# First two token groups transposed on TensorE, the other transposes issued by SyncE, attention units respaced

## Chip, cores and metric

The kernel runs on one core of one Trainium2 chip. The metric is the device time of one launch in microseconds (us), the median of several runs. Engines in the listings: PE is TensorE (matmuls), PEld its weight loads, DVE is VectorE, ACT is ScalarE, POOL is GpSimd, SP is SyncE. A "q" behind a name (ACTq, SPq) is the engine's instruction queue issuing a DMA. L213 is line 213 of the kernel; the change adds lines, so line numbers differ between the two kernels.

## The reference, cut to what matters

Four layers over x of shape 1 x 2048 x 1024, bf16: A, B, A, B, each behind a layer norm and added back to x.

```python
# A: linear attention, 32 heads of 32
q, k, v = split(layernorm(x) @ wqkv)               # 1024 -> 3 x 1024
phi = lambda t: where(t > 0, t + 1, exp(t)) + 1e-6
kv, z = sum_s(phi(k) * v), sum_s(phi(k))           # per head
x = x + ((phi(q) @ kv) / (phi(q) @ z + 1e-6)) @ wo
# B: gated block, F = 3584
x = x + ((h @ w_gate) * (h @ w_up)) @ w_down       # h = layernorm(x)
```

## The kernel before

2048 tokens are 16 tiles of 128, in four groups (g = 0 to 3) of four tiles. The matmuls of this kernel contract over the partitions, so each normalised tile `xn` (tokens on partitions) has to be transposed into `xT` (features on partitions), and each attention output tile `onat` into `oT`. All these transposes are DMAs issued from ScalarE's queue:

```python
def transpose_tile(src, dst):
    nc.scalar.dma_start_transpose(out=dst, in_=src)

def phi(ps, dst):                       # evicts a k or q output
    e = eb[phis[0] % 3]; phis[0] += 1
    nc.scalar.activation(out=e, in_=ps[:], func=ACT.Exp)
    nc.vector.tensor_scalar(out=e, ...)                 # min, add
    nc.vector.scalar_tensor_tensor(out=dst, in0=ps[:], in1=e, ...)

def mm_tile():                          # four PSUM banks for matmul outputs
    return psum.tile([P, NB], F32, tag="mm", bufs=4, name="ps")

def kv_tile():                          # four banks, one buffer
    return psum.tile([P, KD, ZS], F32, tag="kv", bufs=1, name="kv")
# ... cut
def layer_A(li):
    ones()
    if li == 0:
        for t in range(TPG):
            ln_stats(t)
            if t > 0: ln_apply(t - 1)
        ln_apply(3)
        for t in range(TPG):
            tx(t, 0)()                  # DMA transpose of tile t
            k_unit(t, 0)()              # 8 matmuls, then phi
        # ... main: the other k, v and kv units of group 0
        do(weave(main, norm_fill(1, 1, True), 1, 1))
    # ... cut: kv groups 1 to 3, q groups 0 and 1
    do(kv_group(3) + [kv_unit(NT - 1)])
    load_gu(0); load_gu(1)
    f0 = o_fill(0)                      # o units and oT transposes of group 0
    do(weave(q_group(2), [f0[i] for i in (0, 1, 3, 5)], 1, 2))
    do(weave(q_group(3), [f0[i] for i in (2, 4, 6, 7)], 0, 2))
    load_gu(2)
    do(weave(out_group(0), o_fill(1), 0, 1))
    do(weave(out_group(1), [stats_unit(t) for t in range(TPG)] + o_fill(2), 0, 1))
    do(weave(out_group(2), o_fill(3), 0, 1))
    do(weave(out_group(3), norm_fill(0, 0, False), 0, 1))

def layer_B(li):
    load_d()                            # seven 1 MB loads of w_down, on SyncE
    # ... gate/up units, then down units, per group
```

Units are closures that are emitted in list order; each engine works through its own share in that order (at the start of layer 2, below, ScalarE's exps stand behind its transposes until 884.89 us). An o unit is eight small matmuls (128x132) into the single `kv` buffer and a VectorE eviction (L266 before, L281 after). All plain loads are issued by SyncE.

## Time and profile before

The time is 1715.66 us. The floor of TensorE can be worked out from the trace: at full clock eight 128x512 matmuls take 1.727 us and eight 128x132 ones 0.47 us; 7424 of the first and 512 of the second make 1632 us. So about 83 us are lost, and the question is where.

The page of the kernel before: the span, each engine's busy time, TensorE's busy tenths and granted clock in 40 slices, and the chain of waits by engine.

```profile
span 1715.2 us, 18587 instructions
...
PE 1648.8 (96%) x7794; PEld 761.7 (44%) x7952; DVE 538.9 (31%) x963; ACT 246.1 (14%) x418; POOL 53.5 (3%) x150
...
PE   3999998999999999999979999989999999999999
...
PEclk7999999999999999999989999999999999999999
...
PE 94%; DVE 3%; DMA 2%; issue 1%; ACTq 0%; ACT 0%; POOL 0%; POOLq 0%
```

TensorE is the bound; the first slice (43 us) is 30% busy, and there are dents at slices 7, 21 and 27: before layer 1, at the start of layer 2 and before layer 3. TensorE's list of waits in the kernel before: its line and tile, what ended the wait, us in total, how many waits, the longest.

```profile
PE ps L213 <- DMA xT_70<-xn: 24.9, 4, 9.5
PE ps L213 <- ACT H L226: 10.7, 1, 10.7
PE kv L261 <- DVE H L266: 8.1, 8, 2.1
PE ps L301 <- DMA xT_70<-xn: 4.3, 1, 4.3
PE ps L301 <- issue: 4.3, 1, 4.3
```

Five groups of waits, in four places. (For the last line the profile names no releaser; it is the step into layer 3, the same place as the line above it has in layer 1.) The first is the start; its timeline (start us, us, engine, line, operation, and in brackets the idle time before and what ended it):

```profile
6.85 1.42 ACTq L177 DMA_TRANSPOSE xT_70<-xn  x1
...
15.95 3.60 PE L213 MATMUL ps<-W_74,xT_70 128*128 128x512 bf16 x8 [9.51 <-DMA xT_70<-xn]
...
19.58 0.60 ACT L203 ACTIVATE H<-ps 128x512 bf16<-128x512 f32 x1 [17.36 <-PE ps L213]
19.65 1.25 ACTq L177 DMA_TRANSPOSE xT_70<-xn  x1
...
28.56 3.50 PE L213 MATMUL ps<-W_74,xT_70 128*128 128x512 bf16 x8 [9.02 <-DMA xT_70<-xn]
```

The first two transposes take 9 us each to land among the initial loads (the other two 3 us), and each after the first is issued only after ScalarE has done the exp of the tile before. Eight matmuls take 3.5 us here, twice the full-clock time.

The second is the start of layer 2 in the kernel before:

```profile
873.94 1.89 PE L223 MATMUL ps<-W_77,xT_70 128*128 128x512 bf16 x8
...
877.11 7.74 ACTq L177 DMA_TRANSPOSE xT_72<-xn  x4
...
884.89 1.08 ACT L203 ACTIVATE H<-ps 128x512 bf16<-128x512 f32 x2 [65.42 <-DMA xT_72<-xn]
...
885.85 0.69 DVE L205 SCALAR_TENSOR_TENSOR H<-ps,H 128x512 bf16<-128x512 f32 x1
885.86 1.08 ACT L226 CAST H<-ps 128x512 bf16<-128x512 f32 x2
...
886.51 1.44 PE L213 MATMUL ps<-W_74,xT_70 128*128 128x512 bf16 x3 [10.68 <-ACT H L226]
```

In ScalarE's order four transposes stand before the exps. The first k output is complete by 870.65 us (868.76 plus 1.89), but ScalarE waits until 877.11 us for VectorE's normalised tiles, then sits in the four issues, and starts the exp at 884.89. Meanwhile two k and two v outputs fill the four PSUM banks. TensorE's fifth output waits 10.68 us.

The third place is the step into the gate/up matmuls of layers 1 and 3.

```profile
278.91 0.54 DVE L172 TENSOR_SCALAR xn<-X,mv,rstd 128x1024 bf16<-128x1024 bf16 x1
...
280.02 0.37 SPq L95 DMA_DIRECT2D D_78<-in_B_w_down_dram  x1
...
286.06 1.44 PE L301 MATMUL ps<-xT_70,W_74 128*128 128x512 bf16 x3 [4.34 <-DMA xT_70<-xn]
```

The last tile of group 0 is normalised at 279.45 us; its transpose lands 6.6 us later. The fourth place is the attention tail of each A layer, where o units wait for VectorE's eviction of the single kv buffer (L266, 8.1 us in all).

### The profile page before, as it was taken

Reading aid. Unit: us, or ns where it says so; the run is one execution under the profiler, and the core shown is the slowest. Engines: PE = TensorE matmul, PEld = TensorE weight load, DVE = VectorE, ACT = ScalarE, POOL = GpSimd, SP = SyncE. Lnnn points to the kernel's source line nnn. Section 1 sums busy time; section 2 is a strip of 40 time slices with the busy share of each in tenths; the row PEclk is TensorE's granted clock in tenths of the full one; section 3 lists DMA queues with packets and bytes.
Section 4 is the critical chain, followed back from the end, with each engine's and each line's share of the span. In section 5 each row is a group of like instructions: output and inputs, shape, how many; then the busy total and the mean of one; then the engine's idle time right before and its main releaser. Section 6 shows DMA issues by size and latency. Waiting matters only on the chain.

```text
span 1715.2 us, 18587 instructions
## 1 busy us (share of the span) xinstructions
PE 1648.8 (96%) x7794; PEld 761.7 (44%) x7952; DVE 538.9 (31%) x963; ACT 246.1 (14%) x418; POOL 53.5 (3%) x150
## 2 busy tenths in 40 slices
PE   3999998999999999999979999989999999999999
PEld 1444444444444444444434444434444444444444
DVE  2553674321321221132342337742113113111211
ACT  0333300110110011011013332001101101100110
POOL 1100000000000000000110000000000000000000
PEclk7999999999999999999989999999999999999999
DMA  8310447641453164053250015376406424531400
GB/s 263 93 26 13 144 79 207 186 151 46 112 158 99 49 172 147 1 161 109 62 145 16 1 43 148 56 245 174 152 19 172 147 68 116 160 108 63 149 4 22
DMA packets 248900, 183.67 MB, mean 107 GB/s; under 512 B 104432, under 2 KB 239600, under 8 KB 248816
## 3 DMA queue, kind: packets, MB, share of 16 engines
q1 hardware_dynamic: 147440, 157.30, 29.0%
q10 hardware_dynamic: 101376, 25.18, 8.2%
q8 instruction: 62, 1.02, 0.2%
q14 instruction: 22, 0.18, 0.0%
HBM read 153.09 MB, written 4.19 MB: 92 GB/s over the span
## 4 chain that ended last, share of the span: by engine, by line
PE 94%; DVE 3%; DMA 2%; issue 1%; ACTq 0%; ACT 0%; POOL 0%; POOLq 0%
PE ps L301 45%; PE ps L313 22%; PE ps L213 7%; PE ps L250 6%; PE ps L223 6%; PE ps L287 5%; DMA xT_70<-xn 2%; DVE st L158 1%; PE kv L237 1%; PE kv L261 1%; DVE X L279 1%; DVE H L266 1%; ACTq L177 0%; DVE mv L160 0%; DVE den L265 0%
## 5 line engine op out<-in xcount | busy, mean ns | idle before, releaser
L305 DVE TENSOR_TENSOR H<-gs,ps 128x512 bf16<-128x512 f32 x224 | 154.0, 688 | 580.9 <-PE ps L301 559.7
L304 ACT COPY gs<-ps 128x512 f32<-128x512 f32 x224 | 131.0, 585 | 1076.8 <-PE ps L301 951.8
L313 PEld LDWEIGHTS <-H 128*128 128x128 bf16 x1792 | 175.4, 98 | 211.4
L279 DVE TENSOR_TENSOR X<-X,ps 128x512 bf16<-128x512 bf16 x128 | 87.4, 683 | 361.4 <-PE ps L313 330.4
L203 ACT ACTIVATE H<-ps 128x512 bf16<-128x512 f32 x128 | 76.3, 597 | 252.9 <-PE ps L213 89.1
L204 DVE TENSOR_SCALAR H<-H 128x512 bf16<-128x512 bf16 x128 | 37.3, 291 | 203.1 <-ACT H L203 203.1
L301 PEld LDWEIGHTS <-W_74 128*128 128x128 bf16 x640 | 62.9, 98 | 85.7 <-issue 11.5
L301 PEld LDWEIGHTS <-W_75 128*128 128x128 bf16 x640 | 63.2, 99 | 77.6 <-issue 3.6
L301 PEld LDWEIGHTS <-xT_73 128*128 128x128 bf16 x576 | 56.4, 98 | 67.9
L301 PEld LDWEIGHTS <-W_77 128*128 128x128 bf16 x576 | 56.4, 98 | 67.9
L301 PEld LDWEIGHTS <-W_76 128*128 128x128 bf16 x576 | 56.4, 98 | 68.0
L301 PEld LDWEIGHTS <-xT_72 128*128 128x128 bf16 x576 | 56.4, 98 | 68.0
L301 PE MATMUL ps<-xT_70,W_74 128*128 128x512 bf16 x314 | 77.0, 388 | 8.9 <-DMA xT_70<-xn 4.3
L158 DVE BATCH_NORM_STATS2 st<-X 128x6 f32<-128x512 bf16 x128 | 80.9, 674 | 5.1 <-DMA X<-in_A_x_dram 5.1
L301 PE MATMUL ps<-xT_70,W_75 128*128 128x512 bf16 x316 | 76.7, 386 | 0.2
L301 PE MATMUL ps<-xT_70,xT_73 128*128 128x512 bf16 x314 | 75.3, 379 | 0.3
L301 PE MATMUL ps<-xT_70,xT_72 128*128 128x512 bf16 x314 | 75.3, 379 | 0.3
L301 PE MATMUL ps<-xT_71,W_77 128*128 128x512 bf16 x314 | 75.3, 379 | 0.3
L301 PE MATMUL ps<-xT_71,W_76 128*128 128x512 bf16 x310 | 75.1, 379 | 0.5
L287 PEld LDWEIGHTS <-H 128*128 128x128 bf16 x512 | 49.9, 99 | 57.0 <-issue 3.0
L301 PE MATMUL ps<-xT_71,W_75 128*128 128x512 bf16 x314 | 74.6, 379 | 0.4
L301 PE MATMUL ps<-xT_71,W_74 128*128 128x512 bf16 x314 | 74.3, 379 | 0.2
(82 smaller groups left out, 1701.1 us busy)
## 6 DMA issues: line engine op xcount, KB each, us to landing
W_74<-in_B_w_gate_dram SPq DMA_DIRECT2D x20, 1024.0 KB, 5.5
W_75<-in_B_w_up_dram SPq DMA_DIRECT2D x20, 1024.0 KB, 7.7
W_76<-in_B_w_gate_dram SPq DMA_DIRECT2D x18, 1024.0 KB, 5.6
W_77<-in_B_w_up_dram SPq DMA_DIRECT2D x18, 1024.0 KB, 7.7
xT_72<-in_B_w_gate_dram SPq DMA_DIRECT2D x18, 1024.0 KB, 5.3
xT_73<-in_B_w_up_dram SPq DMA_DIRECT2D x18, 1024.0 KB, 7.2
X<-in_A_x_dram SPq DMA_DIRECT2D x16, 256.0 KB, 7.3
out_dram<-X SPq DMA_DIRECT2D x32, 128.0 KB, 1.7
```

The lines of the kernel that those rows point to most:

```text
L158: nc.vector.bn_stats(out=st[:, c, :], in_=X[:, t, c * NB:(c + 1) * NB])
L203: nc.scalar.activation(out=e, in_=ps[:], func=ACT.Exp)
L204: nc.vector.tensor_scalar(out=e, in0=e, scalar1=1.0, scalar2=1e-6, op0=ALU.min, op1=ALU.add)
L213: nc.tensor.matmul(out=ps[:], lhsT=xt[:, k, tl * P:(tl + 1) * P], rhs=wk[n][:, k, :], start=(k == 0), stop=(k == KD - 1))
L223: nc.tensor.matmul(out=ps[:], lhsT=xt[:, k, tl * P:(tl + 1) * P], rhs=wv[n][:, k, :], start=(k == 0), stop=(k == KD - 1))
L250: nc.tensor.matmul(out=ps[:], lhsT=wq[n][:, k, cl * P:(cl + 1) * P], rhs=xT[g][:, k, :], start=(k == 0), stop=(k == KD - 1))
L279: nc.vector.tensor_tensor(out=X[:, t, n * NB:(n + 1) * NB], in0=X[:, t, n * NB:(n + 1) * NB], in1=ps[:], op=ALU.add)
L287: nc.tensor.matmul(out=ps[:], lhsT=oT[(t // TPG) % 2][:, c, tl * P:(tl + 1) * P], rhs=wo[n][:, c, :], start=(c == 0), stop=(c == KD - 1))
L301: nc.tensor.matmul(out=ps[:], lhsT=w[:, k, j * P:(j + 1) * P], rhs=xT[g % 2][:, k, :], start=(k == 0), stop=(k == KD - 1))
L304: nc.scalar.copy(out=gs[:], in_=gp[:])
L305: nc.vector.tensor_tensor(out=hT[:, f, :], in0=gs[:], in1=up[:], op=ALU.mult)
L313: nc.tensor.matmul(out=ps[:], lhsT=hT[:, f, tl * P:(tl + 1) * P], rhs=wd[f][:, n * NB:(n + 1) * NB], start=(f == 0), stop=(f == KF - 1))
```

## The change

Its intent: (1) at the start, transpose groups 0 and 1 on TensorE itself, with a ScalarE copy out of PSUM, instead of waiting for DMAs that stand among the loads; (2) take all other transposes out of ScalarE's queue; (3) spread the o units, transposes and norm units so that none waits for the single kv buffer, and normalise the next layer's first group one output group earlier. The core of the diff:

```diff
-    for k in range(0, KD, 4):
-        load(wk[0][:, k:k + 4, :], wqkv_v[:, k:k + 4, D:D + NB])
+    for k in range(0, KD, 2):
+        load(wk[0][:, k:k + 2, :], wqkv_v[:, k:k + 2, D:D + NB])
 ... (identity added; the mask is built after the first statistics)
     def transpose_tile(src, dst):
-        nc.scalar.dma_start_transpose(out=dst, in_=src)
+        nc.sync.dma_start_transpose(out=dst, in_=src)
 ...
+    def tx_pe(t):
+        def run():
+            if t not in xns:
+                ln_apply(t)
+            src = xns.pop(t)
+            pt = psum.tile([P, KD, P], BF16, tag="mm", bufs=MM, name="pt")
+            for k in range(KD):
+                nc.tensor.transpose(out=pt[:, k, :], in_=src[:, k * P:(k + 1) * P], identity=ident[:])
+            nc.scalar.copy(out=xT[t // TPG][:, :, t % TPG * P:(t % TPG + 1) * P], in_=pt[:])
+        return run
 ... layer_A, li == 0
+            tx_pe(0)()
             for t in range(TPG):
-                tx(t, 0)()
                 k_unit(t, 0)()
+                if t < 3:
+                    tx_pe(t + 1)()
 ...
-            do(weave(main, norm_fill(1, 1, True), 1, 1))
+            fill = []
+            for t in range(TPG, 2 * TPG):
+                fill += [stats_unit(t), apply_unit(t), tx_pe(t)]
+            do(weave(main, fill, 1, 1))
 ... attention tail (the old one is printed above)
+        do([q2[0], kv_unit(NT - 1), q2[1], q2[2], o0[0], q2[3], q2[4], o0[1], t0[0], q2[5], o0[2], t0[1], q2[6],
+            q2[7], o0[3], t0[2], q3[0], q3[1], q3[2], o1[0], t0[3], q3[3], q3[4], o1[1], t1[0], q3[5],
+            q3[6], o1[2], t1[1], q3[7]])
 ... then output groups 0 and 1 with the other o units and the statistics
+        load_gu(2)
+        u = out_group(2)
+        do([t3[0], t3[1], u[0], o3[3], t3[2], u[1], a[0], u[2], t3[3], x[0], u[3], a[1], u[4], x[1], u[5], a[2],
+            u[6], x[2], u[7], a[3]])
+        do([x[3]] + out_group(3))
```

More of the change, by code (lines that the diff above doesn't have):

```diff
@@ L6 @@
 from concourse._compat import with_exitstack
+from concourse.masks import make_identity
 ACT = mybir.ActivationFunctionType
@@ L134, with make_mask @@
     load_o()
-    mask = const.tile([P, ZW], F32, tag="mask", name="mask")
-    nc.gpsimd.memset(mask[:], 0.0)
-    for b in range(HC):
-        nc.gpsimd.memset(mask[32 * b:32 * b + 32, 32 * b:32 * b + 32], 1.0)
-        nc.gpsimd.memset(mask[32 * b:32 * b + 32, P + b:P + b + 1], 1.0)
+    ident = const.tile([P, P], BF16, tag="ident", name="ident")
+    make_identity(nc, ident[:])
     mhalf = const.tile([P, 1], F32, tag="mhalf", name="mhalf")
     nc.gpsimd.memset(mhalf[:], -0.5)
+    mask = const.tile([P, ZW], F32, tag="mask", name="mask")
+    def make_mask():
+        nc.gpsimd.memset(mask[:], 0.0)
+        for b in range(HC):
+            nc.gpsimd.memset(mask[32 * b:32 * b + 32, 32 * b:32 * b + 32], 1.0)
+            nc.gpsimd.memset(mask[32 * b:32 * b + 32, P + b:P + b + 1], 1.0)
     warm = const.tile([P, 1], F32, tag="warm", name="warm")
@@ L186, in tx @@
         return run
-    def tx_group(g, slot):
-        return [tx(g * TPG + tl, slot) for tl in range(TPG)]
+    def tx_pe(t):
[8 more added lines that the diff above has]
+        return run
     def mm_tile():
@@ L355, in layer_A @@
     def layer_A(li):
-        ones()
         if li == 0:
@@ L362, in layer_A @@
             ln_apply(3)
+            ones()
+            make_mask()
+            tx_pe(0)()
             for t in range(TPG):
-                tx(t, 0)()
                 k_unit(t, 0)()
+                if t < 3:
+                    tx_pe(t + 1)()
             ts = range(TPG)
@@ L371, in layer_A @@
                     main.append(kv_unit(t - 1))
-            do(weave(main, norm_fill(1, 1, True), 1, 1))
+            fill = []
+            for t in range(TPG, 2 * TPG):
+                fill += [stats_unit(t), apply_unit(t), tx_pe(t)]
+            do(weave(main, fill, 1, 1))
         else:
+            ones()
             do(weave(kv_group(0), norm_fill(3, 3, False), 1, 2))
@@ L378, in layer_A, with o, to @@
         do(q_group(1))
-        do(kv_group(3) + [kv_unit(NT - 1)])
+        do(kv_group(3))
         load_gu(0)
         load_gu(1)
-        def o_fill(g):
-            o = [o_unit(t) for t in range(g * TPG, (g + 1) * TPG)]
-            tr = [to_unit(t) for t in range(g * TPG, (g + 1) * TPG)]
-            return [o[0], o[1], tr[0], o[2], tr[1], o[3], tr[2], tr[3]]
+        def o(g):
+            return [o_unit(t) for t in range(g * TPG, (g + 1) * TPG)]
+        def to(g):
+            return [to_unit(t) for t in range(g * TPG, (g + 1) * TPG)]
         def out_group(g):
             return [u for t in range(g * TPG, (g + 1) * TPG) for u in (out_unit(t, 0), out_unit(t, 1))]
-        f0 = o_fill(0)
-        do(weave(q_group(2), [f0[i] for i in (0, 1, 3, 5)], 1, 2))
-        do(weave(q_group(3), [f0[i] for i in (2, 4, 6, 7)], 0, 2))
+        o0, t0, o1, t1, o2, t2, o3, t3 = o(0), to(0), o(1), to(1), o(2), to(2), o(3), to(3)
+        q2, q3 = q_group(2), q_group(3)
+        do([q2[0], kv_unit(NT - 1), q2[1], q2[2], o0[0], q2[3], q2[4], o0[1], t0[0], q2[5], o0[2], t0[1], q2[6],
+            q2[7], o0[3], t0[2], q3[0], q3[1], q3[2], o1[0], t0[3], q3[3], q3[4], o1[1], t1[0], q3[5],
+            q3[6], o1[2], t1[1], q3[7]])
+        s = [stats_unit(t) for t in range(TPG)]
+        a = [apply_unit(t) for t in range(TPG)]
+        x = [tx(t, 0) for t in range(TPG)]
+        u = out_group(0)
+        do([u[0], o1[3], t1[2], u[1], u[2], o2[0], t1[3], u[3], u[4], o2[1], u[5], u[6], o2[2], u[7]])
+        u = out_group(1)
+        do([t2[0], t2[1], t2[2], u[0], o2[3], u[1], t2[3], s[0], u[2], o3[0], u[3], s[1], u[4], o3[1], u[5], s[2],
+            u[6], o3[2], u[7], s[3]])
         load_gu(2)
-        do(weave(out_group(0), o_fill(1), 0, 1))
-        do(weave(out_group(1), [stats_unit(t) for t in range(TPG)] + o_fill(2), 0, 1))
-        do(weave(out_group(2), o_fill(3), 0, 1))
-        do(weave(out_group(3), norm_fill(0, 0, False), 0, 1))
+        u = out_group(2)
+        do([t3[0], t3[1], u[0], o3[3], t3[2], u[1], a[0], u[2], t3[3], x[0], u[3], a[1], u[4], x[1], u[5], a[2],
+            u[6], x[2], u[7], a[3]])
+        do([x[3]] + out_group(3))
     def layer_B(li):
```

## The prediction

> What bounds it now. TensorE: 96% of the 1715.2 us span in the page, 94% of the chain of waits. At full clock eight 128x512 matmuls take 1.727 us in the timeline (0.216 each), eight 128x132 ones 0.47. So 7424 of the first and 512 of the second need 1632 us. The other 83 us are TensorE idle or at half cadence (0.427 us a matmul). From its timeline:
> (a) Layer 0 start: the first 32 matmuls of k end at 45.4 us; 6.9 us of work. Waits on xT transposes by DMA: 24.9 us in the list of waits. ScalarE issues each transpose behind the exp of the tile before, and the first two take 9 us to land among the weight loads.
> (b) Attention tail, each A layer: waits for the eviction L266 of 0.34, 1.39, 2.06, about 0.3 us, 0.49 in the last kv unit, about 1.5 us of half clock: some 6 us each.
> (c) Into layers 1 and 3: 4.3 us for the last xT_70 transpose, then half clock: 6.9 and 6.0 us.
> (d) Layer 2 start: 10.7 us idle. ScalarE sits in four transpose issues (877 to 885 us) before it can evict the PSUM banks; then 2.7 us at half clock.
> The last 3.5 us are the final add and store.
>
> What the change does.
> (a) 64 TensorE transposes, 0.06 to 0.11 us each (estimate from the 128x132 matmuls; the Trainium skill, "TensorE: Matmul & The Clock Gate", Part 4, says they don't engage the clock gate; no trace here shows it). A tile costs about 0.6 us plus one ScalarE copy, estimated at 1.05 us from 0.585 for 128x512. xn of tile 0 is there at 6.8 us, tile 1 at 11.5, tiles 2 and 3 at 13.4 and 14.7. Per tile transpose, copy, eight matmuls: 3.6 us warm, 5.5 cold. The 32 matmuls end at 22 to 29 us instead of 45.4; I take 20 saved. The second group adds 2.6 us of transposes and about 1.7 us of waiting for its first normalised tile: net gain 16.
> (b) o units spread. An in-order model with the trace's durations gives 5.3 us of idle for the old order (trace 4.5), 1.9 for the new, at the third o unit. With kv and half clock: 5.4 saved per layer, 10.8 in all. VectorE is nearly full in the two q groups.
> (c) LN transposes are issued a group earlier, ending some 10 us before need: all 12.9 saved.
> (d) ScalarE is free, but VectorE still has its clump of statistics and applies until 878.6. The first bank comes free at 879.7, so 4 us of idle stay, and the half clock: 6.6 saved.
> Issue costs on SyncE (1.25 us a transpose) are off the path; loads are prefetched over 27 us ahead.
>
> Sum: 16 + 10.8 + 12.9 + 6.6 = 46 us, nearly all of it on the critical path. Predicted 1670 us, 1660 to 1681. Faster by over 2% (below 1682): 0.90; same 0.09; slower 0.01.
>
> What would show it: first 32 k matmuls done at 22 to 29 us; transposes of 0.06 to 0.11 us; no wait on xT_70 at layers 1 and 3; 3 to 5 us idle at layer 2's start, ended by VectorE's phi; under 2.5 us of idle in each tail.
>
> What would make it wrong: the clock at half through the start (+6); transposes queueing behind 1 MB loads on SyncE's one queue, delaying the first output group or holding VectorE at onat (+5 a layer); SyncE blocked by a load's buffer wait before a needed transpose; at layer 2, applies waiting for xn buffers (+4).

## The result, and the profile after

The changed kernel takes 1659.54 us (1659.04 to 1660.28, 4 runs) against 1715.66 us; the ratio is 0.9671, 95% interval 0.9654 to 0.9688. Ratios here are the mean time of one kernel's fast runs over that of the other's of the same rounds, so not quite the ratio of the medians quoted. That is a gain of 56.1 us in the medians and of 57.6 us in the two profiled runs. I had forecast a gain of 46 with a range that ended at 1660: the direction and size class were right, the time lies just below the range.

The page after:

```profile
span 1657.6 us, 18876 instructions
...
PE 1643.1 (99%) x8016; PEld 761.1 (46%) x8016; DVE 537.5 (32%) x963; ACT 254.1 (15%) x426; POOL 53.7 (3%) x152
...
PE   8999999999999999999999999999999999999999
...
PEclk9999999999999999999999999999999999999999
```

The dents are gone and the clock is full in every slice. TensorE's list of waits after; the transpose waits and the 10.7 us have no counterpart:

```profile
PE ps L228 <- ACT xT_70 L203: 4.5, 4, 1.1
PE kv L276 <- DVE H L281: 2.6, 2, 1.3
PE pt L202 <- DVE xn L178: 2.0, 3, 1.3
...
PE kv L252 <- DVE H L220: 0.8, 2, 0.5
```

The gain can be placed exactly by reading the start of the same matmul in both TensorE timelines. The fourth column is the difference, the fifth what the stretch since the row above gave.

| Point | before | after | gained so far | in this stretch | predicted |
|---|---|---|---|---|---|
| the first 32 k matmuls done | 45.43 | 21.25 | 24.18 | 24.18 | 20 |
| first k matmul of group 1 | 67.59 | 46.68 | 20.91 | -3.27 | -4.3 |
| first k matmul of group 3 | 154.21 | 133.30 | 20.91 | 0 | 0 |
| output groups of layer 0 done | 281.56 | 255.11 | 26.45 | 5.54 | 5.4 |
| layer 1, ninth gate/up output begun | 302.41 | 268.92 | 33.49 | 7.04 | 6.9 |
| first k matmul of layer 2 | 868.76 | 835.27 | 33.49 | 0 | 0 |
| first k matmul of its group 1 | 911.32 | 865.48 | 45.84 | **12.35** | **6.6** |
| output groups of layer 2 done | 1125.42 | 1073.91 | 51.51 | 5.67 | 5.4 |
| layer 3, ninth gate/up output begun | 1145.34 | 1087.72 | 57.62 | 6.11 | 6.0 |
| end | 1715.2 | 1657.6 | 57.6 | 0 | 0 |

(For "done" in the kernel before, the last eight matmuls start at 279.83 and 1123.69 us, plus 1.73.) Two places differ from the prediction: the start (two rows, by 4.2 us and 1.0 us) and the start of layer 2 (by 5.75 us). The rest is within 0.3 us.

The start, after:

```profile
6.76 0.62 PE L202 MATMUL pt<-ident,xn 128*128 128x128 bf16 x8 [0.28 <-DVE xn L178]
...
7.42 1.01 ACT L203 COPY xT_70<-pt 128x1024 bf16<-128x1024 bf16 x1 [5.19 <-PE pt L202]
8.48 1.90 PE L228 MATMUL ps<-W_74,xT_70 128*128 128x512 bf16 x8 [1.10 <-ACT xT_70 L203]
```

A transposed tile costs 0.62 us on TensorE and 1.01 us of copy (I had estimated 0.6 and 1.05), and eight k matmuls take 1.90 us: full clock.

The start of layer 2, after:

```profile
840.65 0.58 ACT L241 CAST H<-ps 128x512 bf16<-128x512 f32 x1 [1.13 <-PE ps L238]
...
842.17 1.89 PE L228 MATMUL ps<-W_74,xT_70 128*128 128x512 bf16 x8
842.37 0.58 ACT L241 CAST H<-ps 128x512 bf16<-128x512 f32 x1 [1.14 <-PE ps L238]
...
843.62 5.36 SPq L183 DMA_TRANSPOSE xT_72<-xn  x4
...
845.36 0.69 DVE L220 SCALAR_TENSOR_TENSOR H<-ps,H 128x512 bf16<-128x512 f32 x1
...
846.10 0.41 PE L252 MATMUL kv<-H 128*128 128x132 bf16 x4 [0.31 <-DVE H L220]
```

The fifth output (842.17) starts with no idle before it, although VectorE is done with the first output only at 846.05 us (845.36 plus 0.69). I had expected TensorE to stand idle until then. Of the four banks only that of the first v output had been emptied by 842.17 (L241, 840.65 to 841.23 us), so the fifth output stands in that one. The first wait is the kv unit's, which needs the k values themselves: 0.31 us, then 0.52.

The step into layer 1, after:

```profile
242.10 0.54 DVE L178 TENSOR_SCALAR xn<-X,mv,rstd 128x1024 bf16<-128x1024 bf16 x1
...
253.57 0.37 SPq L96 DMA_DIRECT2D D_78<-in_B_w_down_dram  x1
255.11 1.24 PE L316 MATMUL ps<-xT_70,W_74 128*128 128x512 bf16 x5
```

The last tile is normalised 12.5 us before the first gate/up matmul (242.64 and 255.11 us), and there is no wait.

### The profile page after: what moved, and what is told of

The parts are those of the page before. It is cut to its first block, busy times and chain, and to the rows that moved or that the text cites. A ratio compares the mean times of both kernels' runs of the same rounds, so it can differ in the third digit from the quotient of the medians.

```text
span 1657.6 us, 18876 instructions
## 1 busy us (share of the span) xinstructions
PE 1643.1 (99%) x8016; PEld 761.1 (46%) x8016; DVE 537.5 (32%) x963; ACT 254.1 (15%) x426; POOL 53.7 (3%) x152
## 4 chain that ended last, share of the span: by engine, by line
PE 97%; DVE 1%; ACT 0%; DMA 0%; SPq 0%; issue 0%; POOL 0%; POOLq 0%
PE ps L316 47%; PE ps L328 23%; PE ps L302 7%; PE ps L265 6%; PE ps L238 6%; PE ps L228 6%; PE kv L252 1%; PE kv L276 1%; DVE st L164 1%; DMA X<-in_A_x_dram 0%; ACT xT_70 L203 0%; ACT H L218 0%; SPq L96 0%; PE pt L202 0%; DVE H L281 0%
```

## The experiments

Twelve runs were made (eleven kernels, and the changed kernel once more), all correct by the comparison with the reference (one of them should not have been, see the combination). Where a difference of a few us between kernels from different calls is read, I multiply the difference of their ratios by 1715. The 95% interval of one ratio is 2 to 3 us to either side, so a difference of 2 to 4 us (experiments 4, 7 and 8) rests on what the trace shows and not on the ratios alone.

### 1. ScalarE issues the transposes again

```diff
-        nc.sync.dma_start_transpose(out=dst, in_=src)
+        nc.scalar.dma_start_transpose(out=dst, in_=src)
```

> The changed kernel, with every DMA transpose issued by ScalarE again (TensorE transposes and the new order kept). Theory A (the issuing engine is what freed the start of layer 2: there ScalarE sits in transpose issues while the PSUM banks wait): a TensorE gap of about 10 us with half clock behind it returns at the start of layer 2, that stretch is about 12 us longer, total about 1672 us; perhaps 1 to 3 us more in the two attention tails, where ScalarE's exps now stand behind issues. Rival B (the new order and the TensorE transposes alone account for it, the engine is indifferent): 1659 to 1661 us, no gap.

Measured: 1670.83 us (ratio 0.9741). Theory A holds. In the list of waits of this run stands again:

```profile
PE ps L228 <- ACT H L241: 10.9, 1, 10.9
```

That is the v copy at the start of layer 2; otherwise the list is nearly as after (the tails 2.6 us, so my "1 to 3 more in the tails" did not come). The issuing engine is worth 12 us, all in that place. There is no wait at the transitions: with the new order they don't need SyncE.

### 2. The old order of the attention tail

```diff
-        do([q2[0], kv_unit(NT - 1), q2[1], ...   (new tail)
+        do(kv_group(3) + [kv_unit(NT - 1)])      (the old tail, as printed above)
```

> The changed kernel with the attention tail of both A layers in the old order (transposes stay on SyncE, TensorE transposes stay). Theory A (the order alone removed the tail's eviction waits and the wait for the last normalised tile's transpose): 5.5 us come back in each tail, 7.0 and 6.1 us at the two transitions into the gate/up matmuls, in all 24.4: 1684 us. Rival B (the transition wait was caused by the ScalarE issue and is gone with SyncE): only about 11 us come back, 1670 us.

Measured: 1672.02 us (ratio 0.9746): about 13 us slower than the change (12.5 in the medians), not 24.4. My theory A fell here, rival B (1670) was right. The tail waits for L281 are back (8.4 us in all), but the transitions wait only 1.0 us each. From the timeline of this run:

```profile
256.55 0.54 DVE L178 TENSOR_SCALAR xn<-X,mv,rstd 128x1024 bf16<-128x1024 bf16 x1
...
260.37 7.93 PE L316 MATMUL ps<-xT,W 128*128 128x512 bf16 x35 [1.01 <-DMA xT<-xn]
```

The last transpose lands 3.3 us after its tile is normalised (257.09), against 6.6 us before. So the transition has two cures, and either alone is nearly enough: the new order, or the other queue. Why the queue matters is the next experiment.

### 3. The w_down loads later, with the old order and ScalarE's queue

Base: experiment 5's kernel (start of the change alone), whose transitions wait 3.9 us each (4.3 in the kernel before). There the last transpose lands 6.1 us after its tile is normalised (257.95 to 264.09 us).

```diff
         last = li == 3
-        load_d()
 ...
                 main.append(prefetch(i, last))
+                if i == 0:
+                    main.append(load_d)
```

> The kernel with the start of the change alone (transposes on ScalarE, old order), and the seven 1 MB loads of w_down moved behind the first prefetch of each gate/up stage, some 14 us later. Theory A (in the kernel before, the last xT transpose took over 6 us to land because those loads came through the other queue at the same time): it lands about 3.1 us after its issue, the TensorE wait there falls from about 4 to about 1 us and the half clock goes: 4.5 to 5.5 us less at each transition, 1683 to 1686 us against 1694.1. Rival B (the ScalarE issue or the chain of applies is the cause): 1692 us or more, the wait stays near 4 us.

Measured: 1682.55 us (ratio 0.9806 against 0.9878 of its base: about 12 us gained). Theory A; the excess over its 9 to 11 is within the noise. From the timeline of this run:

```profile
258.28 0.54 DVE L178 TENSOR_SCALAR xn<-X,mv,rstd 128x1024 bf16<-128x1024 bf16 x1
...
262.07 23.25 PE L319 MATMUL ps<-xT,W 128*128 128x512 bf16 x107 [0.98 <-DMA xT<-xn]
```

The transpose lands 3.3 us after its tile is normalised, though ScalarE issues it. So in the kernel before the loads of w_down, coming through SyncE's queue at that moment, doubled the landing time of the one transpose that TensorE was waiting for. The Trainium skill, "DMA: Bandwidth & Descriptors", section "Issuing engines are not separate DMA queues", says that DMAs from different engines run on the same 16 DMA engines and interleave; this pair agrees: 6.1 us with the loads beside it, 3.3 without. In one queue (experiment 2) the loads stand behind the transpose.

### 4. Group 1's transposes by DMA

```diff
-                fill += [stats_unit(t), apply_unit(t), tx_pe(t)]
+                fill += [stats_unit(t), apply_unit(t), tx(t, 1)]
```

> The changed kernel with only the first token group transposed on TensorE; the second group's transposes are DMAs on SyncE behind the initial loads. Theory A (the second group's TensorE transposes only cost: 1.8 us of TensorE and 1.35 us of waiting for its first tile): about 3.2 us faster, 1656.3 us, and no TensorE wait on xT_71. Rival B (the transposes stand behind the remaining loads in the one queue and land late): a TensorE wait on xT_71 of several us near 45 us, total 1661 us or more.

Measured: 1656.60 us (ratio 0.9657). Theory A, to 0.3 us (3.0 us faster in the profiled runs, 2.4 in the ratios): no wait on group 1's xT appears, and the wait of 1.35 us for its first normalised tile is gone from TensorE. The change's transposes of the second group only cost; by then SyncE has issued its last initial load.

### 5. The start alone

The kernel before with tx_pe for groups 0 and 1, the four-piece load and the later mask of the change; old order, ScalarE's queue.

> The kernel before with only the start of the change: two token groups transposed on TensorE, the first weight load in four pieces, mask built later; old order, other transposes on ScalarE. Theory A (the parts are independent): the start is 20.9 us shorter, all else as before, 1694.8 us. Rival B (parts interact, for instance a start that runs ahead of the loads waits later): under 18 us gained, 1698 us or more.

Measured: 1694.12 us (ratio 0.9878). Theory A. The list of waits shows all other waits of the kernel before: 10.5 us at layer 2, 8.3 in the tails, 7.8 at the transitions.

### 6. SyncE's queue alone

The kernel before with the one-line edit of experiment 1 turned round.

> The kernel before with one edit: every DMA transpose issued by SyncE instead of ScalarE. Theory A: the layer 2 start gains its 12 us and the two transitions into the gate/up matmuls gain about 5 us each (as in the run with the old order, where the last transpose landed 3 us after its issue), the tails nothing; at the start of layer 0 the transposes now stand behind the 25 initial loads in SyncE's program, so the first k matmul waits until about 38 us instead of 16 and the first 32 end at 44 to 49 us: 1690 to 1697 us. Rival B (the start becomes the bottleneck): the first 32 end after 55 us, 1703 us or more.

Measured: 1696.05 us (ratio 0.9882), inside theory A's range. From its timeline:

```profile
30.66 11.70 SPq L177 DMA_TRANSPOSE xT<-xn  x4
...
40.84 16.32 PE L213 MATMUL ps<-W,xT 128*128 128x512 bf16 x64 [34.35 <-DMA xT<-xn]
```

The first transposes wait in SyncE's program until the 25 loads are issued; k starts at 40.84 us. The v matmuls begin at 57.00 us, 4.6 later than before. Two of the forecast's parts missed a little: k was to start at about 38 us, and the first 32 k matmuls, expected to end by 49, end at about 50.1 (57.00 less 32 times 0.216). In return the wait of 10.7 us at layer 2 is gone from the list, and the transitions wait 1.1 and 1.0 us. So (1) of the change is what makes (2) free of cost at the start.

### 7. Without the dummy matmuls

```diff
-    for i in range(16):
+    for i in range(1):
         nc.tensor.matmul(out=zps[:], ...
```

> The changed kernel with 1 instead of 16 dummy matmuls before the first transposes. Theory A (the start gained 24 us, more than my 20, because the clock was at full rate from the dummy matmuls on and stayed there through waits of 1.1 us): the first tiles run at half cadence (0.427 us a matmul, transposes near 0.107), the 32 matmuls end 2 to 8 us later, 1662 to 1668 us. Rival B (the first transposes and matmuls bring the clock up by themselves or the start is set by the arrival of X): under 1 us later.

Measured: 1661.65 us (ratio 0.9683; about 2 us slower than the change in the ratios, 3.8 us in the profiled runs, whose spans are 1661.4 and 1657.6). Just under theory A's 1662 to 1668. From its timeline:

```profile
6.82 1.04 PE L202 MATMUL pt<-ident,xn 128*128 128x128 bf16 x8 [5.04 <-DVE xn L178]
...
14.51 3.60 PE L228 MATMUL ps<-W,xT 128*128 128x512 bf16 x8 [1.10 <-ACT xT L203]
...
19.84 1.90 PE L228 MATMUL ps<-W,xT 128*128 128x512 bf16 x8 [1.10 <-ACT xT L203]
```

Two tiles run at half cadence, the third at full. The sixteen dummy matmuls were in the kernel before too, but there TensorE then stood idle for 9.5 us and started at half cadence all the same; only now do they pay.

### 8. PSUM banks in strict rotation

The changed kernel, with the matmul outputs (and the transposes' pt) given four tags of one buffer in turn instead of one tag of four.

```diff
+    turn = [0]
+
+    def mm_tag():
+        turn[0] += 1
+        return f"mm{turn[0] % MM}"
+
     def mm_tile():
-        return psum.tile([P, NB], F32, tag="mm", bufs=MM, name="ps")
+        return psum.tile([P, NB], F32, tag=mm_tag(), bufs=1, name="ps")
```

> The changed kernel with the four PSUM banks of the matmul outputs handed out in strict rotation (four tags of one buffer) instead of by the pool. Theory A (my prediction of 4 us idle at the start of layer 2 assumed rotation; the pool gives the fifth output the bank of the first v tile, which ScalarE frees early): the fifth k/v output waits for VectorE's phi of the first, an idle of about 4 us ended by VectorE appears there, with up to 2.7 us of half clock behind it: 1663 to 1667 us. Rival B (the hand-out is indifferent, the gap vanished for another reason): under 1 us difference.

Measured: 1664.21 us (ratio 0.9694, about 4 us slower than the change; 5.3 us in the profiled runs). Theory A. From its timeline, the fifth and sixth outputs of layer 2:

```profile
845.92 6.30 PE L234 MATMUL ps<-W,xT 128*128 128x512 bf16 x16 [3.76 <-DVE H L226]
```

With rotation my predicted idle is there, 3.76 us and ended by VectorE's phi, and most of the sixteen matmuls behind it run at half cadence (6.30 us; 3.5 at full clock). In the change as built the fifth and sixth outputs start at 842.17 and 843.90 us, when only the banks of the two v tiles are empty; ScalarE has freed both by 842.95.

### 9. Two load pieces instead of four

```diff
-    for k in range(0, KD, 2):
-        load(wk[0][:, k:k + 2, :], wqkv_v[:, k:k + 2, D:D + NB])
+    for k in range(0, KD, 4):
+        load(wk[0][:, k:k + 4, :], wqkv_v[:, k:k + 4, D:D + NB])
```

> The changed kernel with the first weight block loaded in two pieces of 512 KB again instead of four of 256 KB. Theory A (with four pieces eight loads are under way before the two 1 MB blocks behind them, so token tile 2 arrives at 8.80 us instead of 9.55 and the second tile's transpose starts that much earlier): tile 2's statistics start near 9.5 us, the first 32 k matmuls end 0.5 to 1 us later, 1660.0 to 1660.6 us against 1659.5. Rival B (the pieces matter by letting the first k matmuls start before the whole block has landed): k's first tile waits for the weights, 1 us or more later.

Measured: 1660.92 us (1659.71 to 1662.43), against 1659.31 (1659.18 to 1659.70) for the changed kernel run again beside it. The ratios, 0.9676 (0.9663 to 0.9689) and 0.9667 (0.9654 to 0.9680), overlap. Inconclusive: tile 2's statistics start at 9.17 us in the profiled run, but among the runs with four pieces they start anywhere from 8.53 us (experiment 2) to 9.51 (experiment 5). Token arrival varies by that much from run to run. No wait on the weights appears, so rival B is out.

The changed kernel again:

> The changed kernel once more, so that the small differences of the other two kernels are read on one chip: 1658.5 to 1660.5 us by every theory.

### 10. A combination

```diff
             fill: group 1 by DMA, as in experiment 4
-            tx_pe(0)()
-            for t in range(TPG):
-                k_unit(t, 0)()
-                if t < 3:
-                    tx_pe(t + 1)()
+            do([tx_pe(0), k_unit(0, 0), tx_pe(1), k_unit(1, 0), tx_pe(2), k_unit(0, 1), k_unit(2, 0), tx_pe(3)])
-            main = [k_unit(t, 1) for t in ts] + [v_unit(t, 0) for t in ts]
+            main = [k_unit(1, 1), k_unit(3, 0), k_unit(2, 1), k_unit(3, 1)] + [v_unit(t, 0) for t in ts]
 ...
-            ... q2[5], o0[2], t0[1], q2[6], q2[7], o0[3], t0[2], q3[0], q3[1], ...
+            ... q2[5], q2[6], o0[2], t0[1], q2[7], q3[0], o0[3], t0[2], q3[1], ...
```

> A version meant to beat both: the changed kernel with the second group's transposes by DMA on SyncE (3.1 us measured above), the third o unit one q unit later (takes away the 1.29 us wait for the single kv buffer in each tail, 2.6 us), and k units of the second half placed where the first four tiles' ScalarE copies were waited for (the three later waits of 1.1 us each go, about 2.6 us in all). Theory A (each wait is on the critical path and independent): 1659.5 - 3.1 - 2.6 - 2.6 = 1651.2 us. Rival B (the waits move on to VectorE or to the second weight block's arrival): 1654 us or more.

Measured: 1654.40 us (ratio 0.9638). Neither: the start gained nearly what it should (first k matmul of group 1 at 41.20 us against 46.68, so 5.5 of 5.7), but a new wait stood in each tail, in TensorE's list of waits:

```profile
PE kv L276 <- DVE D L220: 3.5, 2, 1.7
```

An o unit waits for a *write of q values* (D, L220). That is the trace of a mistake of mine: q groups 0 and 3 share a buffer (three for four groups), and I had put the first q unit of group 3 ahead of the last o unit of group 0. That o unit then read group 3's values in one of its eight chunks. The comparison with the reference let it pass; the wait gave it away. The time of this kernel is no result.

The mended version gives group 3 the idle xT of group 0:

```diff
-    pqT = [... for i in (2, 3, 4)]
+    pqT = [... for i in (2, 3, 4)] + [xT[0]]
-            phi(ps, pqT[g % 3][:, c, :])
+            phi(ps, pqT[g][:, c, :])
```

(and the same in the o unit's read)

> The combined version mended. In the one before, q group 3 wrote its first chunk over the buffer of q group 0 before the last o unit of that group had read it (my fault: three buffers for four groups; the comparison with the reference let it pass, so that run's result is not the right computation), and that o unit waited 1.74 us for the write. Here group 3 gets a buffer of its own, the idle transposed input of token group 0. Theory A (the 1.74 us waits were this hazard alone): they go in both tails and nothing takes their place, 1654.4 - 3.5 = 1650.9 us. Rival B (VectorE is full in the q groups and the o units wait for it instead): 1653.5 us or more, with waits of over 0.5 us on the eviction.

Measured: 1650.88 us (1650.42 to 1651.41), ratio 0.9625 (0.9612 to 0.9639). Theory A. That it agrees to the digit is luck: the median of the kernel before moved by 1.4 us (1714.88 to 1716.31). This is all that is left in TensorE's list of waits:

```profile
PE ps L228 <- ACT xT L203: 2.2, 2, 1.1
PE zps L156 <- DVE xT L153: 1.2, 1, 1.2
PE kv L252 <- DVE H L220: 0.8, 2, 0.5
```

It is faster than the kernel before by 64 us, and than the change run again by 7 us in the ratios (8.4 in the medians).

## Why the prediction was wrong

The parts and the places of the gain were named rightly, and of the terms that were not zero all four in the tails and transitions held to 0.3 us, but the sum was 10 us short in the medians (46 against 56.1), and the range's lower end missed the measured time by half a microsecond.

- **The step that failed: (d), "The first bank comes free at 879.7, so 4 us of idle stay, and the half clock: 6.6 saved."** Measured: 12.35 us saved, and no idle before the fifth output. The time of the first bank was right: 879.7 less the 33.5 us gained up to there is 846.2, and VectorE freed it at 846.05. What failed is the wait. I assumed that the fifth matmul output takes the bank of the first, in rotation, and so must wait for VectorE's phi. The pool had given it the bank of the first v tile, which ScalarE frees early (by 841.23 us). Experiment 8 shows it: forced into rotation, the kernel shows the idle that I predicted, 3.76 us, with half cadence behind it. The evidence was in the profile before, though by a margin of only 0.03 us: the 10.68 us wait was ended by L226, a v copy, and not by VectorE. I read the length of that wait and not its release.
- **(a) was mis-sized: "I take 20 saved" measured 24.18.** I had two cases, 22 us at full clock and 29 at half, and took a value between. The clock stayed full through waits of 1.1 us, and the end came at 21.25. Experiment 7 puts 2 to 4 us on the clock. Some 0.75 us more I put down to token tile 2, whose statistics start at 8.80 us instead of 9.55 and stand before tile 1's normalisation on VectorE; whether the four load pieces or chance did that is open (experiment 9). The second group's cost was 3.27 us, not 4.3.
- **(b) held**: 5.54 and 5.67 us against 5.4. The model of engines in order put the one remaining wait at the third o unit; it is there, 1.29 us.
- **(c) held in size**: 7.04 and 6.11 against 6.9 and 6.0. That the earlier issue alone accounts for it was incomplete: experiments 2 and 3 show that the wait was half made by the w_down loads in the other queue, and that one queue would have removed most of it without the new order.
- The fear that transposes would queue behind the 1 MB loads on SyncE did not come true in the change: no wait on a transpose is left. It is real where the program order is wrong (experiment 6).

So the 57.6 us of the two profiled runs are: start 20.9, ScalarE's queue at layer 2 12.35, tails 11.2, transitions 13.15. What stays open: by what rule the pool chooses a bank (the traces show only which banks were empty); and when a wait brings the clock down. In the kernel before, half cadence followed the wait of 2.06 us in each tail (eight matmuls in 3.35 and 3.24 us); in experiment 2 the same wait of 2.06 us was followed by eight matmuls in 1.89 us, full rate, in both tails. Of the four runs of experiment 8, too, one took 1661.95 us at a granted clock of 1.000, the others 1664.13 to 1664.67 at 0.998 or 0.999. The Trainium skill, "TensorE: Matmul & The Clock Gate", Part 1, "What's actually happening", says that the activity window is free-running; the two pairs of tails fit that, but no run here tests it.

## What to carry to other kernels

Read what ends a wait as carefully as how long it is: the release names the buffer or queue that a cure has to reach, here a v copy's bank and not the phi's. A DMA that an engine stands waiting for should not share its moment with bulk loads from another queue; ordering them in one queue, or issuing the loads later, halved its landing time here. And before keeping an engine's queue for something else, check what its in-order program puts in front: the same one-line move of the transposes to SyncE gained 12 us at layer 2, cut the waits at the transitions from 4.3 to about 1 us each, and lost 5 at the start until the first group no longer needed it. A wait for a write where only a read should stand, as in experiment 10, is the sign of a wrong order, and a passing comparison does not clear it.

## What the Trainium skill lacked or had wrong

- "TensorE: Matmul & The Clock Gate", Part 4: it gives 275 to 390 ns for a bf16 128x128 transpose and says that the full clock does not engage for transposes. Here eight in a row take 0.62 us, 219 ns recorded for one; in the second token group, amid full-clock matmuls, the next instruction starts 0.46 us after the first of them (29.66 to 30.12 us), which is about 57 ns each. In the run without the dummy matmuls the first eight took 1.04 us. So transposes do run at the full clock when it is up; whether they bring it up themselves is not shown.
- The same page, Part 1, has no case in which one and the same short wait goes both ways. Waits of 1.1 us between 1.9 us of work kept the full clock (start of the change), one of 2.06 us led to half cadence in the kernel before and not in experiment 2.
- "DMA: Bandwidth & Descriptors", "Issuing engines are not separate DMA queues": it says that issuing from several engines only saves the sequencer's issue time. Two costs have no size there: a transpose beside loads from another queue landed in 6.1 to 6.6 us against 3.3, and four transpose issues held ScalarE for 7.7 us while PSUM was full.
- No page says that handing out PSUM banks strictly in turn can cost time when their readers free them at different times; here it cost 3.76 us of idle and the half clock behind it.
